# Reordering small pieces of work between the matmuls of a fused RWKV-6 attention and MLP kernel

## The chip, the cores and the metric

The kernel runs on one core of a Trainium2 chip. The metric is the device time of one execution in microseconds (us). Before the change it is 581.06 us, the median of three runs (580.58 to 582.94). The profile that is read below is of a further execution, whose span from first to last instruction is 579.2 us.

A core has a matrix engine (TensorE, PE in the profile), a vector engine (VectorE, DVE), a scalar engine (ScalarE, ACT), a general engine (GpSimd, POOL) and a queue engine that issues transfers (SyncE, SP). Each works through its own instruction stream in the order in which the program put it there, and they meet at semaphores. So a change of order in the program is a change of what stands behind what on each engine.

## The reference, cut to what matters

```python
batch, n_heads, seq, head_dim = (4, 8, 768, 48)       # attention; all float32

def _attn_ref(r, k, v, w, u):
    for t in range(S):
        cur = einsum('bhd,bhe->bhde', u[None] * kt, vt)
        y[:, :, t] = einsum('bhd,bhde->bhe', rt, state + cur)
        state = wt[:, :, :, None] * state + einsum('bhd,bhe->bhde', kt, vt)

def _moe_ref(x, g_ln, w_ch1, w_ch2):                  # d_model 384, inner size 1536
    mu = mean(x); var = mean((x - mu) ** 2)
    xn = (x - mu) / sqrt(var + 1e-06) * g_ln
    return x + maximum(xn @ w_ch1, 0.0) @ w_ch2       # x: attention output, heads side by side
```

The part with `u` is a step's own term: the sum over d of r·u·k is one number for each step and head, and it scales that step's v. The text calls r·u·k "the own products", their sums over d "the own sums", and the sums times v "the own term".

## The kernel before

Work is cut into eight rounds, two for each batch (halves of 384 steps), and each round into two units of four heads (unit q belongs to round q // 2). Each pass of the main loop, numbered `rnd`, forms the attention of round `rnd` in six levels (`lev` 0 to 5), finishes the outputs of round `rnd - 1` (`old`), and prepares round `rnd + 1` (`new`). One pass of one level is called a slot, with the number `(rnd - 1) * 6 + lev`. The steps of the MLP of earlier rounds are strewn between these pieces so that TensorE has matmuls to do while other engines make the next operands ready.

The pieces that the change moves, and those that meet them (cuts are marked with `# ...`):

```python
def own_products(q, eng):               # r * k, then * u: two passes over 128 x 576
    rk = st[q]["ruk"] = p1.tile([P, TT, NH, D], F32, tag="rk", name=f"rk{q}")  # one buffer
    eng.tensor_tensor(out=rk, in0=nat["k"][q % 2][..., 0:D], in1=nat["r"][q % 2][..., 0:D], op=ALU.mult)
    eng.tensor_tensor(out=rk, in0=rk, in1=u_bc[...], op=ALU.mult)

def own_sums(q):                        # sums over d, on VectorE
    o = st[q]["own"] = p4.tile([P, TT, NH], F32, tag="own", name=f"own{q}")
    DVE.tensor_reduce(out=o, in_=st[q]["ruk"], axis=AX.X, op=ALU.add)

def product_sums(q):                    # the same sums on TensorE (rounds 0 and 1 only)
    ps = ps_t.tile([P, RN], F32, tag="t", name=f"own_ps{q}")
    for pr in pairs:
        for c in range(TT):
            PE.matmul(ps[:, ts(pr * TT + c, 2)], a["ruk"][pr][:, ts(c, P)], sel[:, NP * g + pr], ...)
    ACT.copy(out=..., in_=ps[:, 0 : 2 * NK]...)

def own_term(q, eng):                   # v times the own sums, into vo
    eng.tensor_tensor(out=a["vo"], in0=vn[q], in1=a["own"]..., op=ALU.mult)

def quads(q, lev): ...                  # 24 products k x r of a level into a_ps (48 for both units)
def grow(q, lev, which="rk"): ...       # VectorE: r and k of a unit times decays, in place (rkT)
def keep(rnd, lev): ...                 # VectorE: a_ps into A (lev 5: left to copies of ScalarE)
def squares(q, nm, pr): ...             # VectorE: 32x32 transposes of freshly loaded w, k, r
def ends(q, pr): ...                    # TensorE: k turned (kn_ps), copied by ScalarE

def states(q, tag="a"):                 # kv products into PSUM, then the chain of states
    kv = banks(tag, f"kv{q}")           # PSUM pool "a": two buffers, shared with a_ps and y
    # ... 24 matmuls kv<-v,kn
    # ... VectorE: s = s * decay + kv, 12 small instructions, each after the one before

def outputs(q):                         # 48 small matmuls into y, then x = y + vo on VectorE
    # ...

def norm(rnd):                          # after moments(rnd): mean and variance of x
    ACT.activation(out=rstd, in_=mv[:, :, 1], func=AF.Sqrt, bias=eps)
    DVE.reciprocal(out=rstd, in_=rstd)
    for i in range(TT):
        DVE.tensor_scalar(out=xn, in0=xs[b, f][:, i], ...)    # xn, read by turned_x on TensorE

def fill(until, tasks):                 # spreads tasks evenly over MLP steps, until step `until`
    n = int(until) - done
    m = max(n, len(tasks))
    for i in range(m):
        for t in tasks[i * len(tasks) // m : (i + 1) * len(tasks) // m]:
            t()
        for _ in range((i + 1) * n // m - i * n // m):
            mlp_step()
```

An MLP step is three matmuls of 128x384 (in the trace six, since each float32 matmul is recorded twice): either one block of the inner layer (`h_ps`, read by ScalarE's relu) or three accumulations of an output (`o_ps`). An `h_ps` matmul reads a slice of the weights `w1_sb`, which VectorE rebuilds part by part (`join`) while the first MLP runs; ScalarE does the first half of that work (`begin`).

The main loop, with the lines that matter:

```python
for rnd in range(1, NR + 1):
    for lev in range(NLEV):
        if rnd == 2:
            for q in old if lev < 2 else []:
                (states, outputs)[lev](q)
            if lev < 2:
                mlp_step()
        elif old and lev < 2 * U:
            (states if lev < U else outputs)(old[lev % U])
            if lev >= U and now:
                mlp_step()
        # ... quads, grow, keep of the units of `now`
        if rnd == 1:
            # ... loads
            if lev == 1:
                tasks += each(product_sums, now)
        # ... squares and loads of `new`
        if lev == 3 and rnd > 1:
            # ...
            if rnd > 2:
                moments(rnd - 1)
                tasks += each(norm, [rnd - 1])
        if lev == 4 and rnd > 2:
            tasks += each(turned_x, [rnd - 1], range(KC))
            tasks += each(own_products, new[:1], [POOL])
        if lev == NLEV - 1:
            # ...
            if rnd > 2 and new:
                own_sums(new[0])
            if rnd == 2:
                tasks += each(own_products, new[:1], [POOL]) + each(own_sums, new[:1])
            if rnd >= 2:
                tasks += each(own_term, new[:1], [POOL])
                tasks += each(own_products, new[1:], [POOL])
                tasks += each(own_sums, new[1:]) + each(own_term, new[1:], [POOL])
                if new:
                    tasks += each(totals, [rnd + 1], [POOL])   # products of decays, on POOL
            # ... ends and copies mixed in
        if rnd == 1 and lev < NLEV - 1:
            n = (1, 2, 2, 1, 0, 0)[lev] * NP
            tasks += mixed([begin] * BEGINS[lev], [join] * JOINS[lev], ahead[:n])
        fill(UNTIL[slot], tasks)
```

Of the kernel before, what the change touches and what calls it, by code (L numbers as in the profile page):

```python
# [52 lines left out]
def kernel(  # L53
# [13 lines left out]
    PE, ACT, DVE, POOL, SPO = (  # L67
        InOrder(tc, e) for e in (nc.tensor, nc.scalar, nc.vector, nc.gpsimd, nc.sync)
    )
# [149 lines left out]
    for lev in range(NLEV - 1):  # L219
        n = 1 << lev  # L220
# [228 lines left out]
    def quads(q, lev):  # L449

        n = 1 << lev
        rnd, uu = divmod(q, U)
        if uu == 0:
            ps = ps_a.tile([P, 2, 512], F32, tag="a", name=f"a_ps{rnd}_{lev}")
            a_ps[rnd] = ps[:, :, 0 : W // 2].rearrange("s j (u k t) -> s j u k t", u=U, k=NK)
        K = st[q]["k"]
        R = st[q]["r"].rearrange("p (m q two n) -> p m q two n", m=NM, two=2, n=n)
        for c in range(NK):
            for i in range(2):
                for j in range(2):  # L460
                    m = 2 * c + i
                    rows = ds(HP * j, D)
                    PE.matmul(
                        a_ps[rnd][ds(C * (i ^ j), C), j, uu, c]
                        .rearrange("s (q n) -> s q n", n=n),
                        K[rows, ts(m, C)], R[rows, m, :, 1, :], start=True, stop=True,
                    )

    def grow(q, lev, which="rk"):

        n = 1 << lev
        a = st[q]
        T = (a["T"][lev] if lev else a["w"]).rearrange("p (q two) -> p two q", two=2)
        i, m, Q = "rk".index(which[0]), len(which), W // (2 * n)
        X = a["rk"]
        X = bass.AP(
            tensor=X.tensor, offset=X.offset + n + i * (W - n),
            ap=[list(X.ap[0]), [W - n, m], [2 * n, Q], [1, n]],
        )
        DVE.tensor_tensor(  # L480
            out=X, in0=X, in1=T[:, ds(i, m), :, None].broadcast_to([P, m, Q, n]), op=ALU.mult
        )
# [238 lines left out]
    def mlp_step():  # L721
        nonlocal done
        while mlps:
            if next(mlps[0], mlps) is not mlps:
                done += 1
                return True
            mlps.pop(0)
        return False
# [11 lines left out]
    def mixed(*lists):  # L740
        return [
            t for _, t in sorted(
                (((i + 0.5) / len(l), t) for l in lists for i, t in enumerate(l)),
                key=lambda at: at[0],
            )
        ]

    def each(f, *ranges):
        calls = [()]
        for r_ in ranges:  # L750
            calls = [c + (x,) for c in calls for x in r_]
        return [lambda c=c: f(*c) for c in calls]
# [5 lines left out]
    def units_of(rnd):  # L758
        return [U * rnd + g for g in range(U)] if rnd < NR else []
# [36 lines left out]
    ahead = each(turned, new[:1], "wrk", pairs) + each(turned, new[1:], "wrk", pairs)  # L796
# [60 lines left out]
    ahead = [t for nm in "wkr" for t in each(turned, units_of(2), nm, pairs)]  # L857
    JOINS, BEGINS = (3, 4, 4, 4, 4, 2), (3, 3, 4, 4, 3)
    for rnd in range(1, NR + 1):
        old, now, new = units_of(rnd - 1), units_of(rnd), units_of(rnd + 1)  # L860
        if rnd == 1:
            old = []
        for lev in range(NLEV):
            slot = (rnd - 1) * NLEV + lev
            if rnd == 2:

                for q in old if lev < 2 else []:
                    (states, outputs)[lev](q)
                if lev < 2:
                    mlp_step()  # L870
            elif old and lev < 2 * U:
                (states if lev < U else outputs)(old[lev % U])
                if lev >= U and now:
                    mlp_step()
            for q in now:
                if slot:
                    quads(q, lev)
            for which in ("rk",) if lev < NLEV - 1 else "kr":
                for q in now:
                    grow(q, lev, which)  # L880
            if now:
                if rnd == 1 and lev == 0:
                    totals(rnd, DVE)
                keep(rnd, lev)
            tasks = []
            if rnd == 1:
                if lev < 2:
                    tasks += each(load, new, "kr"[lev], [SPO])
                if lev == 2:
                    SPO.dma_start(  # L890
                        out=u_bc,
                        in_=bass.AP(
                            tensor=u.tensor, offset=u.offset, ap=[[0, P], [D, H], [1, D]]
                        ),
                    )
                    tasks += each(load_v, now, [SPO])
                if lev == 3:
                    tasks += each(load_vx, now, [SPO])
                if lev == 1:
                    tasks += each(product_sums, now)  # L900
                if lev in (4, 5):
                    own_term(now[lev - 4], POOL)
            if rnd == 2 and lev == 0:
                tasks += each(load_v, now)
            if rnd == 2 and lev == 2:
                for q in now:
                    take(DVE, q)
                    tasks += each(load, new[q % U :][:1], "kr")
            if rnd == 2 and lev in (3, 4):
                tasks += each(own_term, now[lev - 3 :][:1], [POOL])  # L910
            if rnd > 2 and lev == 1:
                tasks += each(load, new, ["kr"])
            first = 3 if rnd == 2 else 1
            if rnd > 1 and new and first - 1 <= lev < first + 3:
                m = lev - first
                turns = [(new, "w"), (new[:1], "kr"), (new[1:], "kr")]
                if m >= 0:
                    tasks += each(squares, *turns[m], pairs)
                if m < 2:
                    tasks += each(stage, *turns[m + 1], pairs)  # L920
            if rnd == 2:
                if lev == 0:
                    tasks += each(exchanged, old)
                if lev == 1:
                    tasks += [lambda: moments(1), lambda: norm(1)]
                if lev == 2:
                    tasks += each(turned_x, [1], range(KC))
            elif old and lev < U:
                tasks += each(exchanged, [old[lev]])
            if lev == 3 and rnd > 1:  # L930
                for q in now:
                    load_vx(q)
                for q in new:
                    load_v(q)
                if rnd > 2:
                    moments(rnd - 1)
                    tasks += each(norm, [rnd - 1])
            if lev == 4 and rnd > 2:
                tasks += each(turned_x, [rnd - 1], range(KC))
                tasks += each(own_products, new[:1], [POOL])  # L940
            if lev == NLEV - 1:

                if now:
                    mlp_step()
                if rnd > 2 and new:
                    own_sums(new[0])
                if rnd == 2:
                    tasks += each(own_products, new[:1], [POOL]) + each(own_sums, new[:1])
                if rnd >= 2:
                    tasks += each(own_term, new[:1], [POOL])  # L950
                    tasks += each(own_products, new[1:], [POOL])
                    tasks += each(own_sums, new[1:]) + each(own_term, new[1:], [POOL])
                    if new:
                        tasks += each(totals, [rnd + 1], [POOL])
                if now:
                    tasks = mixed(
                        tasks,
                        each(ends, now, pairs) + each(finish, [2, 2, 4])
                    )
                if rnd == 1:  # L960
                    tasks = [join] * JOINS[lev] + tasks + each(totals, [rnd + 1], [POOL])
            if rnd == 1 and lev < NLEV - 1:

                n = (1, 2, 2, 1, 0, 0)[lev] * NP
                tasks += mixed([begin] * BEGINS[lev], [join] * JOINS[lev], ahead[:n])
                del ahead[:n]
            fill(UNTIL[slot], tasks)
            if lev == (2 if rnd == 2 else 4) and old:
                mlps.append(mlp(rnd - 1))
# [32 lines left out]
```

## Time and profile before

| what | value |
|---|---|
| time, median of three runs | 581.06 us (580.58 to 582.94) |
| span of the profiled execution | 579.2 us |
| mean granted TensorE clock | 0.979 of full |
| TensorE busy from 57.6 to 212.0 us | 142.27 of 154.4 us |
| TensorE busy from 212.0 to 579 us | 363.32 of 367.00 us |
| VectorE busy, whole span | 317.3 us (55%) |
| ScalarE busy, whole span | 168.6 us (29%) |
| GpSimd busy, whole span | 94.5 us (16%) |

The page of the profile gives busy times and their shares of the span, a strip of the span in 40 slices, the chain of work that ended last, and the costliest groups of instructions. Three further views of the trace are used. A list of waits tells for which other engine an engine stood idle, and for how long. A timeline lists instructions in order of time: start, duration, engine, the operation with the tile it writes and those it reads, how many were merged into the row, and in brackets the idle time just before. A table of stretches gives each engine's busy time within a stretch, and the TensorE clock that was granted in it. Two things need care: the end of a matmul is modelled, so two neighbouring rows overlap by a little; and a busy TensorE at half clock looks as busy as one at full clock, so the clock column has to be read with the busy column.

### The profile page before, as it was taken

The page shows a single profiled execution, that of the slowest core. Times are in us where ns is not written, and L with a number is a line of the kernel's source. Part 1 is how long each engine was busy: PE and PEld are TensorE (multiplying, and loading weights), DVE is VectorE, ACT ScalarE, POOL GpSimd, SP SyncE. Part 2 cuts the span into 40 slices and gives each one's busy share as a digit, 9 for nine tenths or more (in the row PEclk, how much of TensorE's full clock was granted, in tenths as well). Part 3 has the DMA queues.
Part 4 walks back from the last instruction along what each step waited for, and adds up shares of the span by engine and source line. Part 5 has one row for each costly group of instructions (what it writes and reads, how often), then busy time and mean ns, then how long its engine had stood idle before and what let it go on. Part 6 is the DMA issues. An engine that isn't in the chain of part 4 may idle for free.

```text
span 579.2 us, 19006 instructions
## 1 busy us (share of the span) xinstructions
PE 560.5 (97%) x8378; PEld 370.7 (64%) x8378; DVE 317.3 (55%) x636; ACT 168.6 (29%) x363; POOL 94.5 (16%) x127
## 2 busy tenths in 40 slices
PE   9999989999979989999999999999999999999997
PEld 6776765666546656666666666666666666666554
DVE  4879888769767754558256654557253531130000
ACT  3576597402340015201241015301331025202200
POOL 6140010204062007100350007020420000000000
PEclk9889799999997989999999999999999999999999
DMA  9848587245564547345343534144000000000000
GB/s 231 194 114 166 124 234 179 53 93 101 147 135 89 132 98 138 68 115 120 95 86 82 134 85 89 36 116 103 15 3 2 15 29 2 1 15 29 0 14 27
DMA packets 109875, 50.78 MB, mean 88 GB/s; under 512 B 92768, under 2 KB 99040, under 8 KB 109792
## 3 DMA queue, kind: packets, MB, share of 16 engines
q1 hardware_dynamic: 107920, 48.98, 37.1%
q8 instruction: 65, 1.06, 0.8%
q10 hardware_dynamic: 1872, 0.59, 0.4%
q14 instruction: 18, 0.15, 0.1%
HBM read 42.76 MB, written 4.72 MB: 82 GB/s over the span
## 4 chain that ended last, share of the span: by engine, by line
PE 81%; DVE 6%; ACT 4%; SPq 3%; DMA 3%; issue 2%; POOL 0%; ACTq 0%; DVEq 0%
PE o_ps L49 30%; PE h_ps L49 27%; PE a_ps L49 10%; PE y L49 4%; DVE rkT L49 3%; PE kv L49 2%; SPq L163 2%; DMA v<-in_v_dram 2%; PE kn_ps L49 2%; PE xT_ps L49 1%; ACT rest L49 1%; PE own_ps L49 1%; SPq L173 1%; PE idle L49 1%; PE r_ps L49 1%
## 5 line engine op out<-in xcount | busy, mean ns | idle before, releaser
L49 PE MATMUL o_ps<-w_sb,h 128*128 128x384 f32 x576 | 201.0, 498 | 1.0 <-ACT h L49 1.0
L49 PE MATMUL h_ps<-xT,w_sb 128*128 128x384 f32 x576 | 197.3, 494 | 0.0
L49 PEld LDWEIGHTS o_ps<-w_sb,h 128*128 128x128 f32 x576 | 107.3, 193 | 67.9 <-issue 3.0
L49 PEld LDWEIGHTS h_ps<-xT,w_sb 128*128 128x128 f32 x576 | 106.7, 191 | 66.7 <-issue 1.2
L49 DVE TENSOR_TENSOR rkT<-rkT,tot 128x768 f32<-128x768 f32 (+1 forms) x96 | 79.3, 867 | 28.3 <-issue 15.5
L49 ACT ACTIVATE h<-h_ps 128x384 f32<-128x384 f32 x96 | 46.8, 488 | 151.3 <-PE h_ps L49 151.2
L49 PEld LDWEIGHTS a_ps<-rkT 48*64 48x64 f32 x4608 | 73.7, 137 | 24.3 <-issue 15.9
L49 PE MATMUL a_ps<-rkT 48*64 48x32 f32 x4608 | 79.1, 222 | 3.7 <-DVE s L49 3.0
L49 DVE TENSOR_TENSOR o<-o_ps,x 128x384 f32<-128x384 f32 x24 | 13.3, 555 | 103.2 <-PE o_ps L49 103.1
L49 POOL TENSOR_TENSOR vo<-v,own 128x576 f32<-128x576 f32 x16 | 19.2, 1203 | 258.5 <-DVE own L49 217.7
L49 DVE SCALAR_TENSOR_TENSOR s<-s,decay,kv 128x48 f32<-128x48 f32 x160 | 29.3, 258 | 33.9 <-PE kv L49 33.9
L49 ACT ACTIVATE rstd<-mv,eps 128x3 f32<-128x3 f32 x8 | 2.4, 296 | 134.8 <-DVE mv L49 134.8
L49 DVE COPY_PREDICATED A<-mask,a_ps 128x768 f32<-128x768 int8 x32 | 38.3, 1195 | 0.0
L49 DVE TENSOR_TENSOR x<-y,vo 128x288 f32<-128x288 f32 x32 | 13.2, 453 | 37.4 <-PE y L49 37.3
L49 ACT ACTIVATE xT<-xT_ps,g_sb 128x384 f32<-128x384 f32 x24 | 13.7, 580 | 55.3 <-PE xT_ps L49 55.3
L49 DVE TENSOR_REDUCE own<-rk 128x12 f32<-128x576 f32 x12 | 8.9, 746 | 20.6 <-POOL rk L49 20.6
L49 DVE TENSOR_SCALAR w_sb<-w_sb 128x384 f32<-128x384 f32 (+1 forms) x48 | 18.6, 388 | 0.8
L49 DVE STREAM_TRANSPOSE rkT<-r_runs 128x384 f32<-128x384 f32 x20 | 15.7, 837 | 4.3 <-DMA r_runs<-in_r_dram 4.3
L49 PEld LDWEIGHTS kv<-v,kn 64*64 64x64 f32 x768 | 12.7, 134 | 8.2 <-issue 6.2
L49 PEld LDWEIGHTS y<-v,A 64*64 64x64 f32 x384 | 13.3, 137 | 7.1 <-issue 4.4
L49 DVE TENSOR_TENSOR rkT<-rkT,wT 128x768 f32<-128x768 f32 x16 | 17.1, 1107 | 0.9 <-PE a_ps L49 0.8
L49 DVE STREAM_TRANSPOSE rkT<-k_runs 128x384 f32<-128x384 f32 x20 | 15.8, 849 | 1.7 <-DMA k_runs<-in_k_dram 1.6
(82 smaller groups left out, 501.4 us busy)
## 6 DMA issues: line engine op xcount, KB each, us to landing
raw<-in_moe_w_ch_dram SPq DMA_DIRECT2D x24, 384.0 KB, 3.7
w_runs<-in_w_dram SPq DMA_DIRECT2D x79, 70.0 KB, 2.1
k_runs<-in_k_dram SPq DMA_DIRECT2D x79, 70.0 KB, 2.0
r_runs<-in_r_dram SPq DMA_DIRECT2D x79, 70.0 KB, 2.0
v<-in_v_dram SPq DMA_DIRECT2D x48, 96.0 KB, 3.0
out_dram<-o SPq DMA_DIRECT2D x24, 192.0 KB, 2.8
nat_r<-in_r_dram SPq DMA_DIRECT2D x42, 96.0 KB, 3.3
nat_k<-in_k_dram SPq DMA_DIRECT2D x42, 96.0 KB, 3.2
```

The costliest lines, as they stand in the source:

```text
L49: return lambda *args, **kw: self.tc.keep_in_program_order(f(*args, **kw))
L163: eng.dma_start(out=t[ds(HP * j + SQ * e, SQ), 0:n], in_=bass.AP(tensor=src.tensor, offset=first + SQ * e, ap=[[NS * D, SQ], [1, n]]),)
L173: eng.dma_start(out=vn[q][:, c], in_=steps(v, q, c))
```

## The change

The change adds no arithmetic and removes none. It moves four kinds of small work in the program's order.

1. The own products of the first unit of round 3 (made in pass 2) are begun in level 4 instead of level 5, and their sums are put at the start of level 5, ahead of that level's transposes, as the later passes have it already. It is for the chain of VectorE and GpSimd that ends pass 2.
2. From pass 3 on, `norm` stands ahead of the transposes (`squares`) of its slot, so that the normalized x is there earlier for TensorE.
3. In pass 1, level 1, the sums that TensorE makes for round 1 (two blocks of six matmuls with a result of two columns) are mixed among the turns and MLP steps of the slot, where they stood together ahead of them.
4. In pass 2, level 1, an MLP step stands between the outputs of the two units, and another after the second, where there was one after both; the count at the end of the slot stays as it was.

```diff
@@ pass 2, levels 0 and 1 @@
                 for q in old if lev < 2 else []:
                     (states, outputs)[lev](q)
-                if lev < 2:
-                    mlp_step()
+                    if lev or q == old[-1]:
+                        mlp_step()
@@ pass 1 @@
-                if lev == 1:
-                    tasks += each(product_sums, now)
@@ level 3 @@
                 if rnd > 2:
                     moments(rnd - 1)
-                    tasks += each(norm, [rnd - 1])
+                    tasks = each(norm, [rnd - 1]) + tasks
             if lev == 4 and rnd > 2:
                 tasks += each(turned_x, [rnd - 1], range(KC))
+            if lev == 4 and rnd > 1:
                 tasks += each(own_products, new[:1], [POOL])
@@ level 5 @@
-                if rnd > 2 and new:
+                if rnd >= 2 and new:
                     own_sums(new[0])
-                if rnd == 2:
-                    tasks += each(own_products, new[:1], [POOL]) + each(own_sums, new[:1])
@@ pass 1, before fill @@
-                tasks += mixed([begin] * BEGINS[lev], [join] * JOINS[lev], ahead[:n])
+                tasks += mixed(
+                    [begin] * BEGINS[lev], [join] * JOINS[lev], ahead[:n],
+                    each(product_sums, now) if lev == 1 else [],
+                )
```

## The prediction

> **What bounds the kernel now.** I read the page first. TensorE (PE) is busy nearly all the time, and the strip shows where it is not, or not at full clock: the first third.
>
> ```profile
> PE 560.5 (97%) x8378; PEld 370.7 (64%) x8378; DVE 317.3 (55%) x636; ACT 168.6 (29%) x363; POOL 94.5 (16%) x127
> ...
> PE   9999989999979989999999999999999999999997
> ...
> PEclk9889799999997989999999999999999999999999
> ```
>
> No work is removed, so only idle time and half-clock time can be won. From 212 us on PE is busy 363.32 of 367.00 us, and the end there is set by a fixed amount of matmuls: what is won before 212 us should move the end by as much. So next I read the list of PE's waits, and then the stretches around them with the granted clock.
>
> ```profile
> PE a_ps L49 <- DVE s L49: 3.0, 1, 3.0
> PE xT_ps L49 <- DVE xn L49: 2.1, 1, 2.1
> PE r_ps L49 <- ACT rkT L49: 1.6, 1, 1.6
> ...
> 168.90:173.80 4.90, 1.02 (x53) 0.88 (x52) 4.90 (x12) 1.25 (x3) 4.59 (x6) 0.97 0.85 156
> 173.80:180.30 6.50, 6.50 (x102) 4.81 (x103) 6.50 (x14) 0.86 (x2) 3.73 (x4) 0.50 0.52 85
> ...
> 207.60:211.10 3.50, 3.50 (x9) 2.25 (x9) 2.38 (x3) 1.14 (x2) 0.00 (x0) 0.51 0.64 156
> ...
> 60.90:67.70 6.80, 6.80 (x22) 4.87 (x22) 6.39 (x12) 0.88 (x3) 0.00 (x0) 0.50 0.69 145
> ```
>
> After the length, each row has busy us of PE, weight loads, VectorE (DVE), ScalarE, GpSimd (POOL), then the clock. Three stretches run at 0.50, and each follows one in which PE was idle or did two-column matmuls. The waits are few, but each is paid twice: as idle time, and as half clock after it. The timeline tells why the longest one is there:
>
> ```profile
> 162.23 0.70 DVE L49 TENSOR_REDUCE own<-rk 128x12 f32<-128x576 f32 x1
> 167.03 0.75 DVE L49 TENSOR_REDUCE own<-rk 128x12 f32<-128x576 f32 x1 [4.11 <-POOL rk L49]
> 167.70 0.31 DVE L49 COPY s<-kv 128x48 f32<-128x48 f32 x2
> 169.69 3.06 DVE L49 TENSOR_TENSOR rkT<-rkT,wT 128x768 f32<-128x768 f32 x2
> 172.68 0.95 DVE L49 TENSOR_TENSOR A<-a_ps,bits 128x768 int32<-128x768 int32 x1
> ...
> 163.00 1.15 POOL L49 TENSOR_TENSOR vo<-v,own 128x576 f32<-128x576 f32 x1 [19.93 <-DVE own L49]
> 165.60 1.40 POOL L49 TENSOR_TENSOR rk<-rk,u_bc 128x576 f32<-128x576 f32 x1
> ...
> 169.88 0.91 PE L49 MATMUL kv<-v,kn 64*64 64x48 f32 x48 [0.90 <-PE h_ps L49]
> 173.78 2.79 PE L49 MATMUL a_ps<-rkT 48*64 48x32 f32 x96 [2.98 <-DVE s L49]
> ```
>
> One reduction on DVE (162.23) releases POOL, POOL makes the second unit's products until 167.0, DVE stands idle 4.11 us for them, and behind its second reduction wait the state chain, the decay products and A, for which PE waits. The first reduction's operand had been ready since 143.1; it only stood behind transposes.
>
> [...]the half-clock stretches begin at about 23.3, 40.4, 60.9, 173.5 and 207.6 us[...]. [...]two decay products take 1.82 us at 129.53, with POOL idle, and 3.06 us at 169.69, beside POOL.
>
> **The change part by part.**
>
> Part 1, own products and sums. POOL made the first products at 138.87 to 143.1 already, so beginning them a level earlier gains nothing; the move of the sum does. It will follow level 5's decay products, which end at 155.7. Then: sum until 156.5, own term on POOL (1.15) until 157.6, the second products (1.41 + 1.40) until 160.5. The second sum stays behind a transpose that waits for its load and ends at 162.2, so it runs without a wait until 162.9. State chain (0.31 + 1.84, together 2.0 by the starts of the rows) until 165.0; decay products beside POOL (3.06) until 168.0; A until 168.9. PE ends its three MLP steps at 168.9, runs the second kv (0.84) until 169.8, and finds all ready. So the 0.90 and 2.98 us of idle go. The a_ps block costs 1.53 instead of 2.79 us, and the o_ps work up to 184.45, now 7.89 us for three MLP steps, costs 6.00 as it does at 252.23. By sums: 168.9 + 0.84 + 1.53 + 6.00 = 177.3 against 184.45. Gain 7.15 us, all of it on PE's path.
>
> Part 2, norm first. In pass 3 PE waits 2.10 us for xn, which stands behind four transposes and an output sum (202.69 to 205.88). Moved ahead, xn starts after ScalarE's root (202.70, 0.30) at about 203.2 and ends at 204.4; PE arrives at 204.5. The half clock from 207.6 to 211.1 goes too. PE from 204.5: turn 0.82 and one MLP step 1.94 until 207.4, where it was 211.5 before. Gain 4.1 us. In later passes PE has no such wait, so I give them 0.
>
> Part 3, spread sums. The 24 recorded two-column matmuls take 3.61 us together (59.15 to 62.76), then half clock stretches the next MLP step from 1.94 to 4.05 us and two turns from 0.82 to 1.36. In the new order PE goes from a_ps (until 59.15) to a turn and then to an MLP step whose three weight slices DVE joins by 59.4, 60.7 and 61.9. So it is done at about 62.6 only, with 1.3 us idle: the sums had hidden that. Adding 1.45 for each half of the sums, 1.94 for each of two steps and 0.35 to 0.4 for each of three turns, the next a_ps begins at 70.6 against 72.49: 1.9 us. ScalarE, idle from 62.96 to 66.84 before, starts its work some 3 us earlier, so the 1.59 us wait for it at 78.68 may go, too. DVE, nearly full from 73.4 to 112, limits the sum to about 3.8 us. [...]if it drops, one window at half rate costs 1.7 us and the whole part is worth 1.2. I take 2.3.
>
> Part 4, a step between outputs. Two waits called issue (1.01 and 0.39 us, at 118.39 and 123.10) follow 192 tiny matmuls in a row, and no other y block of the later passes, where a step stands between, has one. Both should go: 1.4 us for PE. But DVE is nearly full from 122.27 to 147.95, then waits for loads that its own transposes release, and PE waits for it at 154.4 (0.89 us). DVE's first work there follows the a_ps block, which by sums (1.4 + 2.13 + 1.4 + 2.13 + 0.77 after 114.97) reaches its first half at 122.8, later than the 122.2 of before. So PE would gain early and give it back at 142 and 154. I count 0.2 us lost.
>
> Sum: 7.15 + 4.1 + 2.3 - 0.2 = 13.35 us, so 567.7. I take off 0.8 for new small waits behind a busier DVE: 568.5 us.
>
> **The rivals.** First: the stalls move on. With PE 7 us earlier after 169 us, the transposes' loads (issue 181.40 to 190.3, transposes at 191.69 to 194.6) could become the wait. For it: DVE waits for loads at 147 to 162 already. Against it: those loads are released by DVE's own transposes at 180.49, which move as well, and DVE idles 2.62, 1.30 and 2.22 us in 183 to 199. This would leave 4 us of part 1: 572. Second: the clock drops anyway, in other windows, because parts 3 and 4 make idle gaps of 1 to 2 us before 155. [...]against it, the 1.59 us idle at 77 dropped nothing. Two more drops cost about 3.4 us: 572. Third: part 3 frees ScalarE more than I count, and no window drops: 4 us in place of 2.3, 566. Fourth: PE's end is set by something else after 212 us. PE's 99% there speaks against it; it would leave the time within 2%.
>
> **Range and chances.** The limit of 2% is 569.4 us, just above my figure, so faster by over 2% is little better than even: 0.56. If one of the first two rivals holds, it is within 2%: 0.43. Nothing adds work, and 12 us of known loss stand against at most a few new ones: slower 0.01. Range 564 to 573.5: 17 us below the old time if all comes and the first steps gain more, 7.5 if only one of the first two parts comes in full.
>
> **What would show it.** Part 1: the wait of a_ps for s and DVE's wait for rk are gone, and the clock is 1.00 after kv. Part 2: no wait of xT_ps for xn. Part 3: the a_ps block of level 2 begins about 2 us earlier, with a wait of h_ps for w_sb before it; a clock of 0.50 near 64 to 68 shows the bad case. Part 4: no wait called issue at the y blocks, but longer waits of a_ps or kn_ps for rkT before 155. The prediction is wrong if PE is idle more than 2 us between 160 and 212 in a place that had no wait, or if the time from that point to the end differs from before.

## The result, and the profile after

The changed kernel takes 566.92 us, the median of four runs (566.13 to 568.2), beside 582.0 us for four runs of the kernel before, measured with it (580.58 to 583.5). The ratio is 0.9743, with a 95% interval of 0.9708 to 0.9777. The prediction was 568.5 us, range 564 to 573.5, so the figure held.

The profiled execution spans 564.85 us where the one before spanned 579.25: 14.40 us less. Its page, busy time and strips:

```profile
PE 550.5 (97%) x8378; PEld 363.5 (64%) x8378; DVE 315.4 (56%) x636; ACT 168.8 (30%) x363; POOL 92.9 (16%) x127
...
PE   8999998998899999999999999999999999999997
...
PEclk9899999999999999999999999999999999999999
```

PE runs the same 8378 instructions in 10 us less busy time, and it stands idle some 4 us less. Equal work in less busy time is the clock: its mean rose from 0.979 to 0.997, and only one slice of the strip is left below 9. In these two traces half clock (a granted 0.50) lasts 3.41 us or, twice in the trace of before, 6.83. Counted in windows of 3.41 us these are seven before (one each at 23.3, 40.4 and 207.6 us, two each at 60.9 and 173.5) and one after (22.7 to 26.1). Six windows fewer, each worth half its length at 0.50, make an estimated 10.2 us; the prediction's 1.7 us for one window is the same estimate. The list of waits of the kernel after (us in total, times, longest us):

```profile
PE kn_ps L49 <- DVE rkT L49: 1.6, 1, 1.6
PE h_ps L49 <- DVE o L49: 1.4, 1, 1.4
...
PE o_ps L49 <- ACT h L49: 1.0, 1, 1.0
...
PE a_ps L49 <- DVE rkT L49: 1.0, 2, 0.5
...
PE h_ps L49 <- DVE w_sb L49: 0.6, 2, 0.3
...
PE y L49 <- issue: 0.3, 1, 0.3
```

The two longest waits of before, a_ps for s and xT_ps for xn, are gone. New ones stand at the top: h_ps for DVE's output sum is new, and kn_ps for rkT grew from 0.9 to 1.6. They stand in pass 2, where part 4 is; the experiment on part 4 tells which of them it makes. The wait for w_sb is the one that the prediction asked for in part 3. The table of stretches of the kernel after, over the three places that ran at half clock before (after the length: busy us of PE, weight loads, DVE, ACT, POOL, then clock, DMA share, GB/s):

```profile
61.60:69.20 7.60, 7.60 (x46) 5.61 (x44) 6.92 (x14) 5.45 (x13) 0.00 (x0) 1.00 0.88 189
...
167.20:169.50 2.30, 2.30 (x146) 2.26 (x145) 1.32 (x9) 0.49 (x1) 0.33 (x2) 1.00 0.74 139
169.50:175.50 6.00, 6.00 (x22) 3.34 (x25) 6.00 (x11) 0.86 (x2) 2.33 (x2) 1.00 0.84 156
...
195.50:202.40 6.90, 6.90 (x35) 4.23 (x27) 5.87 (x9) 1.63 (x3) 0.00 (x0) 1.00 0.51 113
```

All are at 1.00 with PE busy throughout. (They lie some us earlier than before, as the work has moved.) The timeline of the kernel after shows why the long wait is gone:

```profile
153.63 0.74 DVE L49 TENSOR_REDUCE own<-rk 128x12 f32<-128x576 f32 x1
...
154.45 1.15 POOL L49 TENSOR_TENSOR vo<-v,own 128x576 f32<-128x576 f32 x1 [14.07 <-DVE own L49]
...
160.51 0.70 DVE L49 TENSOR_REDUCE own<-rk 128x12 f32<-128x576 f32 x1
161.12 0.31 DVE L49 COPY s<-kv 128x48 f32<-128x48 f32 x2
...
166.10 0.94 DVE L49 TENSOR_TENSOR A<-a_ps,bits 128x768 int32<-128x768 int32 x1
...
167.20 0.92 PE L49 MATMUL kv<-v,kn 64*64 64x48 f32 x48
167.93 1.57 PE L49 MATMUL a_ps<-rkT 48*64 48x32 f32 x96
169.43 6.07 PE L49 MATMUL o_ps<-w_sb,h 128*128 128x384 f32 x18
```

The first reduction runs at 153.63 instead of 162.23, POOL follows at once, and the second reduction at 160.51 has no bracket: DVE no longer stands idle for POOL. A ends at 167.0, before PE begins the second kv, and a_ps follows kv without a gap. The three MLP steps behind it take 6.07 us; the prediction had 6.00 in place of 7.89.

To account for all 14.40 us, the span is cut at starts of PE blocks that occur in both kernels. The cuts are: the first a_ps of level 1 in pass 1; the first kv of pass 2; the first kn_ps of pass 2; the first o_ps after the first unit's outputs in pass 3 (part 1 of the prediction reckoned up to these outputs); the first h_ps after the turn of xT in pass 3; the end.

| from, to | before, us | after, us | gain | what changed there |
|---|---|---|---|---|
| 0 to a_ps, pass 1 level 1 | 57.55 | 56.51 | 1.04 | nothing: no changed instruction yet |
| to kv, pass 2 | 48.08 | 45.84 | 2.24 | part 3 |
| to kn_ps, pass 2 | 48.78 | 50.03 | -1.25 | part 4, and more (see no4) |
| to o_ps after outputs, pass 3 | 31.52 | 24.60 | 6.92 | part 1 |
| to h_ps after xT, pass 3 | 31.43 | 27.01 | 4.42 | part 2 in pass 3 |
| to the end | 361.89 | 360.86 | 1.03 | part 2 in passes 4 to 6 |

### The profile page after: what moved, and what is told of

It reads as the page before. It is cut to its first block, busy times and chain, and to the rows that moved or that the text cites. A ratio compares the mean times of both kernels' runs of the same rounds, so it can differ in the third digit from the quotient of the medians.

```text
span 564.9 us, 19007 instructions
## 1 busy us (share of the span) xinstructions
PE 550.5 (97%) x8378; PEld 363.5 (64%) x8378; DVE 315.4 (56%) x636; ACT 168.8 (30%) x363; POOL 92.9 (16%) x127
## 4 chain that ended last, share of the span: by engine, by line
PE 84%; DVE 6%; ACT 4%; DMA 2%; SPq 2%; issue 2%; ACTq 0%; DVEq 0%
PE o_ps L49 33%; PE h_ps L49 28%; PE a_ps L49 10%; PE y L49 4%; PE kv L49 2%; DVE w_sb L49 2%; ACT rest L49 2%; PE kn_ps L49 2%; SPq L163 1%; DMA nat_r<-in_r_dram 1%; PE xT_ps L49 1%; DVE rkT L49 1%; PE own_ps L49 1%; PE k_ps L49 1%; PE r_ps L49 1%
## 5 line engine op out<-in xcount | busy, mean ns | idle before, releaser
L49 PE MATMUL o_ps<-w_sb,h 128*128 128x384 f32 x576 | 197.6, 492 | 1.1 <-ACT h L49 1.0
L49 PEld LDWEIGHTS o_ps<-w_sb,h 128*128 128x128 f32 x576 | 105.3, 190 | 66.5 <-ACT h L49 2.3
L49 DVE TENSOR_TENSOR rkT<-rkT,tot 128x768 f32<-128x768 f32 (+1 forms) x96 | 76.4, 837 | 26.9 <-issue 16.8
L49 PEld LDWEIGHTS a_ps<-rkT 48*64 48x64 f32 x4608 | 72.5, 135 | 21.0 <-issue 10.7
L49 PE MATMUL a_ps<-rkT 48*64 48x32 f32 x4608 | 77.9, 220 | 1.1 <-DVE rkT L49 1.0
L49 DVE TENSOR_SCALAR w_sb<-w_sb 128x384 f32<-128x384 f32 (+1 forms) x48 | 20.4, 425 | 0.8
L49 POOL TENSOR_TENSOR rk<-nat_k,nat_r 128x576 f32<-128x576 f32 x10 | 15.6, 1555 | 6.5 <-DMA nat_r<-in_r_dram 6.5
```

What stands on the lines that cost most here:

```text
L49: return lambda *args, **kw: self.tc.keep_in_program_order(f(*args, **kw))
```

## The experiments

Four of the experiments (no1, no2, no3, no4) take one part back each; the others ask why a part works or fails. In every edit below, `-` is the changed kernel and `+` the experiment. Times are medians, with range and number of runs; the ratio is to the kernel before on the same chip. The number that separates the theories is often not the whole time but the length of a segment in the trace, because the clock of the first 55 to 60 us, which no edit but the last one touches, differs by chance from run to run (more on it below). A segment is read from one execution of each kernel.

**Part 1 undone (no1).**

```diff
@@ level 4 @@
-            if lev == 4 and rnd > 1:
+            if lev == 4 and rnd > 2:
                 tasks += each(own_products, new[:1], [POOL])
@@ level 5 @@
-                if rnd >= 2 and new:
+                if rnd > 2 and new:
                     own_sums(new[0])
+                if rnd == 2:
+                    tasks += each(own_products, new[:1], [POOL]) + each(own_sums, new[:1])
```

> The changed kernel with part 1 undone (the first own sum of pass 2 back behind that level's transposes). Theory (the sum's place holds up the chain of VectorE and GpSimd): the waits of kv and a_ps near 167 to 172 us come back with 0.9 and 3.0 us, the clock falls to 0.50 after them, and the time is 7 us above the changed kernel, 574. Rival (the wait that is left before 154 us, and not this order, sets the time there): PE arrives late anyway and the time is within 2 us of the changed kernel, 567 to 569.

574.26 us (573.72 to 575.2, 4 runs), ratio 0.9902 (0.9866 to 0.9938). By the two medians the part is worth 7.3 us. The stretches and the timeline of this kernel:

```profile
171.50:173.30 1.80, 0.14 (x9) 0.17 (x13) 1.80 (x5) 0.00 (x0) 1.62 (x3) 1.00 1.01 188
173.30:180.10 6.80, 6.80 (x103) 4.92 (x101) 6.80 (x13) 0.86 (x2) 3.62 (x3) 0.50 0.54 92
```

```profile
166.42 0.75 DVE L49 TENSOR_REDUCE own<-rk 128x12 f32<-128x576 f32 x1 [4.12 <-POOL rk L49]
...
173.16 2.68 PE L49 MATMUL a_ps<-rkT 48*64 48x32 f32 x96 [1.71 <-DVE s L49]
```

The first row is the gap: PE works 0.14 us in 1.80. The whole pattern returns: DVE idle 4.12 us for POOL, PE idle behind it, then half clock. PE's wait is 1.71 instead of 2.98 us; a half-clock window at another place (156.3 to 159.7) had already delayed PE in this execution. From the last a_ps of pass 2 to the kv of pass 4 the kernel needs 72.19 us, the changed one 66.15: 6.04 us by the trace.

**Only the sum moved (sumonly).** The prediction said that beginning the products a level earlier gains nothing. Here they are begun in level 5, directly ahead of the moved sum.

```diff
@@ level 4 @@
-            if lev == 4 and rnd > 1:
+            if lev == 4 and rnd > 2:
                 tasks += each(own_products, new[:1], [POOL])
@@ level 5 @@
+                if rnd == 2:
+                    own_products(new[0], POOL)
                 if rnd >= 2 and new:
                     own_sums(new[0])
```

> The changed kernel, with the first own products of round 3 begun in level 5 again as before, directly ahead of their sum, which stays at the start of level 5. Theory (of part 1 only the place of the sum counts, since GpSimd stood idle and made the products early in either program): within 0.7 us of the changed kernel in one group, a ratio of 0.975 to 0.981 to the kernel before, with GpSimd's products still near 136 us. Rival (the earlier beginning counts): 2 us or more above.

567.67 us (566.74 to 568.57, 6 runs), ratio 0.9792 (0.9762 to 0.9822). From the kv of pass 2 to that of pass 4 the trace has 110.16 us, the changed kernel 110.89. So the sum's place is the whole of part 1. POOL begins the products at the same point as in the changed kernel, 33.81 us behind the kv of pass 2 in both (at 136.16 there), although they stand a level later in the program:

```profile
138.51 2.12 POOL L49 TENSOR_TENSOR rk<-nat_k,nat_r 128x576 f32<-128x576 f32 x1
```

**Part 1 undone, but the idle gap filled (no1_warm).** The wait is paid twice, the prediction said: as idle time and as half clock. Here PE multiplies zeros during the wait (a helper that the kernel has already; nothing reads the result), so that the wait stays and only the clock's part can go.

```diff
  (on top of "part 1 undone")
+            if rnd == 3 and lev == 1:
+                warm(12, "t")            # 128x384 matmuls of zeros, 2.86 us
             for q in now:                # quads, grow, keep
```

> Part 1 undone, and twelve blocks of 128 columns of matmuls of zeros (2.6 us) put where PE idles then, between the second unit's kv and the a_ps block of level 1 of pass 3; their result is not used. Theory (the wait costs twice, as idle time and as half clock after it): the idle time stays filled, the clock stays at 1.00, and the time is 2.5 to 3.2 us below that of part 1 undone alone, 571 to 572. Rival (idle time is the only cost): no gain, 574 or more.

571.39 us (569.31 to 572.65, 6 runs), ratio 0.9876 (0.9835 to 0.9916). In the same group the changed kernel, run again (after2), took 567.52 us (565.93 to 569.01, 6 runs), ratio 0.9803 (0.9765 to 0.984):

> The changed kernel again, as the control for the other runs of this group. Every theory expects a ratio of 0.974 to 0.977 to the kernel before, some 566 us.

The timeline and one stretch of no1_warm:

```profile
167.68 2.86 PE L49 MATMUL idle<-nought 128*128 128x384 f32 x8
170.64 1.60 PE L49 MATMUL a_ps<-rkT 48*64 48x32 f32 x96
```

```profile
170.70:178.20 7.50, 7.50 (x118) 4.79 (x118) 7.50 (x16) 0.86 (x2) 3.79 (x4) 1.00 0.49 75
```

The a_ps block takes 1.60 instead of 2.68 us, and the stretch behind it is at 1.00. From that a_ps to the kv of pass 4 it is 45.35 us, as in the changed kernel (45.31), against 48.59 with part 1 undone alone. So the half clock costs 3.24 us of part 1, where the prediction had 1.26 + 1.89 = 3.15. The idle time is the rest, some 4 us: 3.87 by the medians of no1_warm and after2, 4.00 by the traces (from the kv of pass 2 to that of pass 4 no1_warm has 114.89 us, the changed kernel 110.89). The segment decides here: the ratios of the two kernels, 0.9902 and 0.9876, have intervals that overlap.

**Part 2 undone (no2).**

```diff
-                    tasks = each(norm, [rnd - 1]) + tasks
+                    tasks += each(norm, [rnd - 1])
```

> The changed kernel with part 2 undone (norm behind the transposes again, in all passes). Theory: one wait of about 2 us of xT_ps for xn in pass 3, half clock for one window after it (1.9 us), and 0.35 us in each of three later passes, whose first turn took 0.75 us instead of 0.38: 4.1 + 1.0 = 5 us above the changed kernel, 572. Rival (the later passes gained by something else, and pass 3 has slack after part 1): 2 us or less, 569.

574.31 us (570.57 to 575.86, 4 runs), ratio 0.9891 (0.9848 to 0.9935). The difference of 7.4 us to the changed kernel is more than part 2 is worth: the first segment of the profiled execution (575.2 us) is 60.52 us, 4 us of chance. By segments, kv of pass 2 to kv of pass 4 takes 114.71 instead of 110.89 us (3.8), and the rest to the end 352.63 instead of 351.61 (1.02). Its timeline in pass 3 and in a later pass, with the weight loads (PEld) of the latter, and the stretch behind the first wait:

```profile
200.75 1.44 PE L49 MATMUL xT_ps<-ident,xn 128*128 128x128 f32 x6 [2.10 <-DVE xn L49]
...
265.03 0.91 PE L49 MATMUL xT_ps<-ident,xn 128*128 128x128 f32 x3
265.61 0.14 PEld L49 LDWEIGHTS xT_ps<-ident,xn 128*128 128x128 f32 x1 [0.25 <-DVE xn L49]
265.78 2.10 PE L49 MATMUL o_ps<-w_sb,h 128*128 128x384 f32 x6
```

```profile
202.20:205.70 3.50, 3.50 (x7) 1.65 (x7) 1.91 (x3) 0.81 (x2) 0.00 (x0) 0.51 0.56 152
```

and the same two places in the kernel after:

```profile
194.28 1.26 DVE L49 TENSOR_SCALAR xn<-x,mv,rstd 128x384 f32<-128x384 f32 x3
195.52 0.87 PE L49 MATMUL xT_ps<-ident,xn 128*128 128x128 f32 x6
...
257.54 0.55 PE L49 MATMUL xT_ps<-ident,xn 128*128 128x128 f32 x3
257.92 2.10 PE L49 MATMUL o_ps<-w_sb,h 128*128 128x384 f32 x6
```

In pass 3 the wait of 2.10 us is back, and half clock behind it (0.51). In the later pass there is no bracket at a PE row in either, but from the turn's start to the next block are 0.75 us in the one and 0.38 in the other: three matmuls merged into one row waited for their thirds of xn. One such wait, 0.25 us, shows at the weight load of the third; the rest shows only in the starts of the next rows.

**Part 3 undone (no3), and undone with its clock mended (no3_warm).**

```diff
@@ no3, pass 1 @@
+                if lev == 1:
+                    tasks += each(product_sums, now)
                 ...
-                    each(product_sums, now) if lev == 1 else [],
@@ no3_warm: as no3, but with zeros (1.5 us) between the two blocks of sums @@
+                    tasks += [lambda: product_sums(now[0]),
+                              lambda: (warm(6), product_sums(now[1]))]
```

> The changed kernel with part 3 undone (the sums that TensorE makes for round 1 together again). Theory: half clock after the block of sums in most executions, 2 to 3.3 us above the changed kernel, 569 to 570. Rival (the gain before 115 us was chance of the clock's window, not of the order): within 1 us, 566 to 568.

> Part 3 undone, with six blocks of 128 columns of matmuls of zeros (1.3 us, result not used) between the two blocks of six sums, so that PE does real-sized work among them. Theory (the block of sums costs by the half clock after it): the clock stays at 1.00 after the sums, and the time is 1 to 2 us below part 3 undone alone, in spite of 1.3 us more work: 0.5 to 1.3 us above the changed kernel. Rival (it costs because it holds ScalarE's and VectorE's work up): 1 us above part 3 undone alone.

no3 took 568.55 us (567.31 to 570.82, 4 runs), ratio 0.9806 (0.9766 to 0.9846); no3_warm 567.06 us (566.02 to 569.64, 6 runs), ratio 0.9788 (0.9755 to 0.9822), as much as sumonly in its group. By its time no3 lies between its theory and its rival, so the traces have to decide. The profiled execution is the slowest of the four; the fastest has a mean clock of 0.996, which by an estimate (0.4% of its span, 564.9 us, at 1.7 us lost for each window) leaves room for one or two half-clock windows in all where the profiled one (0.984) has five, so the drop behind the sums need not be as long each time. The stretch of no3 behind the sums, and the sums themselves:

```profile
60.38 3.36 PE L49 MATMUL own_ps<-sel,ruk 128*128 128x2 f32 x24
63.60 4.19 PE L49 MATMUL h_ps<-xT,w_sb 128*128 128x384 f32 x6
```

```profile
62.20:69.10 6.90, 6.90 (x23) 4.97 (x23) 6.49 (x12) 1.30 (x4) 0.00 (x0) 0.52 0.66 143
```

and the same place in the timeline of no3_warm:

```profile
57.73 1.50 PE L49 MATMUL own_ps<-sel,ruk 128*128 128x2 f32 x12
59.09 1.54 PE L49 MATMUL idle<-nought 128*128 128x384 f32 x4
60.47 1.39 PE L49 MATMUL own_ps<-sel,ruk 128*128 128x2 f32 x12
61.73 2.18 PE L49 MATMUL h_ps<-xT,w_sb 128*128 128x384 f32 x6
```

24 two-column matmuls in a row keep PE busy for 3.4 us, and the next MLP step runs at half clock: 4.19 us for what takes 2.18, in a stretch (61.7 to 69.2) with a clock of 1.00, when 1.5 us of zeros stand between the sums. The segment of part 3 is 48.14 us in no3, 46.09 in no3_warm, 45.84 in the changed kernel. So holding the clock with zeros wins 2.05 of the 2.3 us, although the zeros take 1.5 us of PE themselves. What the order would be worth at full clock without them was not measured. That the drop is no chance of one execution shows in all thirteen traces: half clock between 57 and 75 us stands in the two kernels that have the sums together without zeros (before, 0.50 from 60.9 to 67.7; no3, 0.52 from 62.2 to 69.1), and in none of the other eleven. In the same way the windows between 160 and 215 us stand only where the waits are: behind part 1's in before and no1, behind part 2's in before and no2.

**Part 4 undone (no4).**

```diff
                 for q in old if lev < 2 else []:
                     (states, outputs)[lev](q)
-                    if lev or q == old[-1]:
-                        mlp_step()
+                if lev < 2:
+                    mlp_step()
```

> The changed kernel with part 4 undone (outputs of both units of round 1 together, one MLP step after them). Theory (VectorE's stream from 120 to 152 us sets the pace there, and part 4 starts it later): the waits called issue come back, but the time is equal or up to 0.6 us lower than the changed kernel, 566.3 to 567. Rival ([...]this is lost for good): 1 to 2 us above, 568 to 569.

565.88 us (565.6 to 567.22, 6 runs), ratio 0.9759 (0.9727 to 0.979), beside 0.9743 and 0.9803 for the two measurements of the changed kernel: no difference that these runs resolve. In the trace the issue wait at y returns, the wait of h_ps for the output sum is gone, and kn_ps waits as long as with part 4:

```profile
114.80 0.26 PE L49 MATMUL y<-s,rkT 48*64 48x48 f32 x2 [1.21 <-issue]
...
151.18 0.87 PE L49 MATMUL kn_ps<-ident,rkT 128*128 128x128 f32 x6 [1.52 <-DVE rkT L49]
```

```profile
152.60:156.10 3.50, 3.50 (x9) 1.96 (x8) 2.56 (x4) 0.55 (x2) 2.77 (x3) 0.51 0.59 159
```

Yet kv to kn_ps of pass 2 takes 49.33 us, 0.7 less than in the changed kernel's first trace and 0.26 less than in its second (49.59). Closing the issue wait brings nothing: what PE gains there it loses again in the wait for the output sum. The longer wait at kn_ps is not part 4's, as it stands here too. Nor is the whole loss of 1.25 us in the table: without part 4 the segment is still 0.55 longer than the 48.78 of before. PE comes to this pass earlier than before, and that may be why; it wasn't tried. Half clock (0.51) follows the wait at kn_ps here and not in the changed kernel (1.00 from 151 to 156 us), behind a wait as long (1.55 us): nothing in the order tells which of the two happens.

**DVE relieved in pass 2 (pool, pool_no4).** If DVE's stream is what takes back part 4's gain, taking work off it should let the gain through. Round 2's own products (1.41 + 1.40 us each on POOL in place of DVE) go to POOL, their sums into gaps of DVE; pool_no4 also undoes part 4.

```diff
             if rnd == 2 and lev == 0:
+                own_products(now[0], POOL)
+                own_sums(now[0])
+                own_products(now[1], POOL)
@@ rnd == 2 and lev == 2 @@
-                    take(DVE, q)             # own_products and own_sums on DVE
@@ rnd == 2, level 1, after the outputs @@
+                if lev == 1:
+                    own_sums(now[1])
```

> The changed kernel, with round 2's own products moved from VectorE in level 2 of pass 2 to GpSimd in level 0, and their sums into gaps of VectorE in levels 0 and 1. Theory (VectorE's stream from 120 to 152 us is what PE waits for): the waits of h_ps for the output sum (1.4 us) and of kn_ps for rkT (1.5 us) go or shrink, 2 to 3 us below the control, 563 to 564. Rival (the loads of r and k set the pace there, issued one after the other by the queue engine): the first wait goes and the second grows by as much, within 0.7 us of the control.

> As the kernel before this one, with part 4 undone as well. Theory (part 4 delays VectorE's stream and is worth nothing where that stream sets the pace; with the stream relieved, PE sets it, and the two waits called issue cost their 1.4 us): 1 to 1.5 us above the kernel with part 4. Rival (part 4 is worth nothing either way): equal within 0.5 us.

pool: 567.27 us (566.53 to 569.49, 6 runs), ratio 0.9806 (0.9768 to 0.9845): no gain. pool_no4: 565.55 us (563.03 to 567.61, 6 runs), ratio 0.9766 (0.9724 to 0.9807). The timeline of pool, and a line of pool_no4:

```profile
119.36 1.42 POOL L49 TENSOR_TENSOR rk<-nat_k,nat_r 128x576 f32<-128x576 f32 x1
119.66 4.01 DVE L49 TENSOR_TENSOR rkT<-rkT,tot 128x768 f32<-128x768 f32 x2 [1.49 <-PE a_ps L49]
...
121.65 0.90 PE L49 MATMUL a_ps<-rkT 48*64 48x32 f32 x48 [1.36 <-DVE rkT L49]
...
123.73 1.50 PE L49 MATMUL a_ps<-rkT 48*64 48x32 f32 x48 [1.18 <-DVE rkT L49]
```

```profile
121.55 2.77 DVE L49 TENSOR_TENSOR rkT<-rkT,tot 128x768 f32<-128x768 f32 x2
```

In pool the two waits at which it was aimed, h_ps for the output sum and kn_ps for rkT, are gone. But POOL's products ran beside the two decay products that PE waits for, which took 4.01 us where they take 1.83 in the changed kernel (at 120.01, with POOL idle). PE waited 1.36 and 1.18 us, and half clock followed (123.2 to 130.0). So neither the theory nor the rival of pool came true: both waits went, and new ones took the gain. In pool_no4 the decay products take 2.77 us, and an MLP step stands between a_ps of level 1 and a_ps of level 2 to cover them: part 4 had taken that step away to put it between the outputs. From the kv of pass 2 to that of pass 4, pool takes 111.75 us, pool_no4 107.92, the changed kernel 110.89 and 110.41. So with POOL's help part 4 is harmful in these traces, and the expectation for pool_no4, that it would be slower than pool, fell too; the two windows of half clock, an estimated 3.4 us, are most of the difference. By the times alone the two stay unresolved, as their intervals overlap.

**A version faster than the change (pool_no4_w).** What is left below full clock lies in the first 45 us. There the two-column sums of round 0 stand between waits. Zeros are put around them, eight 128x128 blocks in all:

```diff
  (on top of pool_no4)
         if lev == 1:
+            warm(2)
             product_sums(u0)
+            warm(3)
@@
     product_sums(u1)
+    warm(3, "t")
```

> Part 4 undone and round 2's own products on GpSimd, and eight more blocks of 128 columns of zeros in the first 45 us, around the sums of round 0. Theory (the two blocks of sums there lower the clock in most executions, by one to three windows): no half clock before 50 us, level 1 of pass 1 begins at 56 to 57 us in place of 56.5 to 59.2, the runs lie closer together, and the time is 1 to 2 us below the same kernel without the zeros, 563.5 to 564.5. Rival (the zeros delay VectorE's first levels by as much as they save): equal, 565 to 566.

561.88 us (561.71 to 566.14, 6 runs, five of them below 563.1), ratio 0.9706 (0.9668 to 0.9744). In its group sumonly, which equals the changed kernel, has 0.9792 (0.9762 to 0.9822), so it is faster than the change, by 5 to 6 us. Its profiled execution has a mean clock of 1.000; the stretch of it where most others drop:

```profile
15.00:58.00 43.00, 39.33 (x1023) 29.95 (x1021) 35.98 (x82) 28.03 (x61) 6.98 (x10) 1.00 0.67 151
```

That the zeros bring the gain is not shown. Level 1 of pass 1 begins at 58.36 us in this trace, not at the expected 56 to 57, and at 58.76 in sumonly's, which has three windows of half clock there: PE is busy 2.7 us less but idle 2.3 us more, 2.08 of it in one wait called issue. Of the 5.25 us between the two traces 4.30 lie between the kv of pass 2 and that of pass 4 (105.86 against 110.16), where pool_no4 differs from the change and no zeros stand. What goes with the zeros is a steadier clock: 0.999 or more in five of six runs, where pool_no4 has 0.988 to 0.997 and takes the longer the lower it is (563.03 us at 0.997, 567.61 at 0.988). This may be the 3.7 us between the medians of the two kernels, which come from two groups.

## Why the prediction was right

- **What bounds it.** "What is won before 212 us should move the end by as much": from the kv of pass 4 to the end it is 352.63 us before and in no2, and 351.61 or 351.62 in the eleven traces with part 2. It held, but for 1.02 us that were won behind that point. The prediction named a different time there as a sign that it is wrong; that sign came, in this size, by part 2 in the later passes.
- **Part 1: 7.15 predicted, 6.92 measured** (6.04 where it alone is undone). The sum's place is the cause (sumonly), the halves are some 4 us of idle time and 3.24 of half clock (no1_warm). The second half was reckoned at 3.15.
- **Part 2: 4.1 predicted, 4.42 measured in pass 3, and 1.03 in the later passes where 0 was predicted.** The failed term is "In later passes PE has no such wait, so I give them 0". It was read from the list of waits and from brackets; each of three passes held 0.30 to 0.37 us of waits within a merged row, each too small to be listed. no2 has them back: 1.02 us.
- **Part 3: 2.3 predicted, 2.24 measured, but by another share.** The first segment's 1.04 set aside, the a_ps of level 2 begins 2.17 us earlier (72.42 before, 69.21 after), for which the prediction had 1.9; PE's idle time for the weight slices is 0.63 us (0.28 and 0.35), where it had 1.3. PE's wait for ScalarE falls from 1.59 to 0.30, as it thought possible, so that PE is 3.46 us ahead at the h_ps behind it (79.07 and 74.57). It gives 1.22 of that back before the kv of pass 2, in part to a new wait of 0.49 for ScalarE's h. The clock drop that the prediction feared near 64 to 68 us was its author's estimate, as no trace of before has that order; it did not come (1.00 from 61.6 to 69.2). no3_warm, with the old order and a held clock, has all of the part but 0.25: what makes it is that the sums no longer drop the clock.
- **Part 4 and the small waits: 0.2 + 0.8 lost predicted, 1.25 measured.** That part 4 gains nothing was right: no4 equals the change in time. One place was wrong: "PE would gain early and give it back at 142 and 154". In place of 142 it became the output sum at 135.49; the wait at kn_ps came, but no4 has it too, so it belongs to the small waits of an earlier PE. Of the 1.25 us, 0.7 at most goes with part 4:

```profile
135.49 4.14 PE L49 MATMUL h_ps<-xT,w_sb 128*128 128x384 f32 x12 [1.36 <-DVE o L49]
...
152.38 0.87 PE L49 MATMUL kn_ps<-ident,rkT 128*128 128x128 f32 x6 [1.55 <-DVE rkT L49]
```

- **The rest, 1.04 us, no term had.** It lies ahead of the first changed instruction. The kernel before had half clock at 23.3 to 26.7 and at 40.4 to 43.8 us, the one after only in the first place. The kernels of the experiments, with no edit there, spread over more than that (below), so it is chance and not the change.
- **The rivals.** The stalls did not move on to the transposes' loads (first): between 161 and 213 us no PE row of the kernel after has a bracket. The clock did not drop in other windows (second), but that is luck in part: it did at 156.3 in no1 and at 152.6 in no4, behind a wait that the changed kernel has as well. That "each is paid twice" is therefore too strong; a wait can be paid twice. And what ScalarE's earlier start won at its best place, 3.46 us, did not last (third), and the end is PE's (fourth).

By the sum of steps: 7.15 + 4.1 + 2.3 - 0.2 - 0.8 = 12.55 us predicted; 6.92 + 4.42 + 1.03 + 2.24 - 1.25 = 13.36 measured, and 1.04 of chance. No term misses by more than 1.03 us, and the misses cancel in part. Whether the gain is over 2% was called little better than even, and so it is: 0.9743 (0.9708 to 0.9777) says yes, and 0.9803 (0.9765 to 0.984), when the same kernel was measured again, leaves it open.

## What to carry to other kernels

Where the matmul engine is nearly full, look for the few waits and for the clock column behind each: here waits of some 4 us (part 1) and of 2.10 us (part 2 in pass 3) cost 3.24 and an estimated 1.7 us more in half clock, and where part 1's wait could not go, zeros in its place saved those 3.24 us (no1_warm). Before moving a step to close a gap, ask what that step was covering where it stood. And to see small waits, compare the starts of neighbouring rows in two traces: the list of the matmuls' waits leaves them out.

## What the runs showed of the hardware

- **Chance in the clock is as large as a part of the change.** In the 5 us from 20 us on, the same part of the program ran at 0.64 in the changed kernel run again (after2, first row) and at 1.00 in no1_warm (second row), whose edit lies 140 us later:

```profile
20.00:25.00 5.00, 4.77 (x110) 4.69 (x111) 3.86 (x4) 0.73 (x3) 0.84 (x2) 0.64 0.76 140
```

```profile
20.00:25.00 5.00, 4.76 (x140) 4.16 (x141) 4.99 (x5) 1.95 (x7) 1.79 (x2) 1.00 0.68 124
```

  The first segment, the same work in all kernels but the last, took 55.27 to 60.52 us, and it goes with the number of half-clock windows in it: 55.3 to 56.4 us with none, 56.2 to 56.5 with one, 57.6 with two, 58.6 to 59.2 with three, 60.5 with four. The spread, 5.25 us of 567 or 0.9%, is more than part 3 is worth (2.24), and about as much as part 2 (4.42 + 1.03). The kernel before varied from 575.1 to 583.2 us within one group, with the granted clock from 0.991 to 0.974.
- **The clock dropped behind a busy PE, too.** In no3 PE was busy without a gap through 24 two-column matmuls (3.36 us), and the clock dropped to 0.52 behind them, as it did before behind the idle time of 168.9 to 173.8 us (0.50). Behind other waits it stayed at 1.00: 1.55 us at kn_ps in the changed kernel, 1.59 us at 78.68 before (1.00 from 74 to 80). What decides it isn't shown. Blocks of 64x48 and 48x32 ran at 1.00 (167.20 to 169.50 after); these 2.3 us don't show how it would be in a longer row of them.
- **Order on one engine.** Before, DVE ran the first own sum at 162.23, though its operand was there at 143.1 and DVE stood idle 5.8 us between 149 and 162 for loads of the transposes ahead of it; put ahead of them, it ran at 153.63.
- **Two engines side by side.** Two decay products on DVE took 1.83 us in the changed kernel with POOL idle (120.01), and beside POOL's work 2.77 in pool_no4 and 4.01 in pool.
- **What stayed open.** The waits called issue (1.21 us in no4, and one of 2.08 us at 33.3 in the last version) come mostly within long rows of small matmuls. What they are wasn't tried. They come and go in equal instructions: in pass 2 pool_no4 has one of 1.45 us at y, its rows of y take 4.64 us with it, and an a_ps block behind them takes 2.01; pool_no4_w, the same there, has no such wait, 2.99 us and 1.60. These two places make up the 2.06 us by which their segments from the kv of pass 2 to that of pass 4 differ (107.92 and 105.86). Which part of 2.77 or 4.01 us is contention, and which the order in which DVE and POOL happened to start, wasn't separated either.
